# When queued work is issued around attention visits: turns and loads behind odd visits, queue rates that grow, x rows stored later

## The chip, the cores and the metric

The program runs on one core of one Trainium2 chip. The metric is the device time of one execution, in microseconds. Three runs of the kernel before took 1429.32, 1425.75 and 1430.16 us (median 1429.32). Beside them stands one profiled execution.

## What is computed

Attention with RMS-normalised queries and keys, over 8 batches of 12 heads, 448 rows of 64 numbers, followed by a feed-forward block with a squared ReLU on 3584 rows of 768 numbers:

```python
def rmsnorm(x, g):
    rms = np.sqrt(np.mean(x * x, axis=-1, keepdims=True) + 1e-06)
    return x / rms * g
q_n, k_n = (rmsnorm(q, g_q), rmsnorm(k, g_k))
scores = (1.0 / np.sqrt(q.shape[-1])) * np.matmul(q_n, k_n.transpose(0, 1, 3, 2))
scores = scores - np.max(scores, axis=-1, keepdims=True)
attn = np.exp(scores)
attn = attn / (np.sum(attn, axis=-1, keepdims=True) + 1e-09)
attn_out = np.matmul(attn, v)
x = attn_out.transpose(0, 2, 1, 3).reshape(3584, 768)
h = np.maximum(x @ w_in, 0.0)          # w_in: 768 x 2048
out = h * h @ w_out                    # w_out: 2048 x 768
```

## The kernel before

**Two streams in one program.** Attention is done for 48 pairs of heads (two heads fill the 128 partitions), six pairs for each batch. The feed-forward part (FFN) is done in four units `u`, each for two batches, that is twelve pairs: unit 0 runs while pairs 13 to 24 are attended, unit 1 with pairs 25 to 36, unit 2 with 37 to 47, and unit 3 runs alone at the end. `ffn(u)` (L925) is a generator. It issues a product, and yields its cost. `run(until)` (L1498) draws from it until the costs reach `until`, and `place(u, x)` (L1484) says how far the FFN shall be when a visit to a pair is issued. TensorE's order is thus written by hand: some FFN products, a visit, some FFN products. All engines execute in the order of issue, each its own, and so does SP, which issues all DMAs of the steady part.

**A unit.** A unit has four blocks. From unit 1 on a block begins with deep products (`deep_products`, L989, matmuls on L1018), seven products of four steps at cost 9 or 6 each, and goes on with second products (`second_products`, L1142, matmuls on L1134 and L1196), steps of cost 10 or 20. The weight pieces for the deep products (in_sb, out of in_deep in DRAM) come through `load_piece` (L873, DMA on L885) into a ring of a little over four products, about four products ahead. The weights of the second products (out_sb) come through `load_out` (L892, DMA on L895), 1.5 MB each.

**Visits.** Pairs up to 24 are visited twice each. From pair 25 on a pair is `whole` (L275): one visit, `visit_whole(i)` (L1676), which issues the scores of pair i (L433, and L444 for even i), their exponentials on ACT (`weigh`, L449, on L452) and the products of pair i - 1 with its values (L548, L569). The scores go to a few banks in turn, so a score waits until the exponential that reads its bank is done. There are three visits for each block: within the deep products, behind the first steps of the second products, and near the end of the second products. In unit 1 the odd pairs 27 and 33, in unit 2 the odd pairs 39 and 45, are at the second of these places. At pairs 25 and 37 a new unit begins, and `drain()` empties the queues ahead of the visit.

**Queued work.** What a visit needs later is put into two queues of small functions, `tasks` and `pool_tasks`. After each FFN step, `run` calls `run_tasks(most, to_send)` (L1517): it takes `most` functions (2 if the step's cost is over 10, otherwise 1) from each queue. `held` stops it: from the fourth of the deep products on for `pool_tasks`, and from the start of the seventh for `tasks`, until the second products are under way (L1190, L1207), which is just ahead of the second visit of a block. In front of each visit `run_all()` (L1523) empties both queues, held or not. Among the tasks are:

- `turn_blocks(i + 1, x)` (L362) for k (x = 1) and q (x = 0): DVE transposes (L365), for q followed by a scaling on ACT (L367), which make kT and qT of the next pair. They are put into the queue half-way between two visits (L1736), and so is `load_qk(i + 4)` (L1552), four or eight DMAs.
- `prepare(i + 3)` (L1659): the squares on ACT (L179), their sums on DVE (L192, L195), then, through `pool_tasks`, the powers and the scaling on POOL (L202, L217), and for q a way through DRAM (`store_q`, `load_blocks`), since the transposes want another layout. For even visits it is put into the queue later.
- the inversion of the sums (`invert_both`, L615), `load_v`, and `additions` (L457), six POOL operations (L471) for each pair.

**Transfers.** The DMAs of q and k go into one more queue, `transfers`, while FFN steps are drawn. `follow_transfers` (L320) sends them: 2 and one more for each eight in the queue per step in the first unit, `most` later; after the first unit `run_all` sends all that are left. `ensure` sends those that an operation needs.

**x rows.** A finished pair of a later unit, xT, is stored in DRAM (x_rows) if the forms of the unit before are still in use (`settle`, L719, DMA on L725), and loaded again by `bring` (L794). The store goes into `later`, a list that counts FFN steps (`follow_loads`, L1447): here 2.

Of the kernel before, what the change touches and what calls it, by code (L numbers as in the profile page):

```python
# [5 lines left out]

# [217 lines left out]
def program(ctx, tc, rows, v, g, wide, ones, moe_w_in, moe_w_out, out, shift):  # L224

    nc = tc.nc
# [38 lines left out]
    values, turned, through = {}, {}, {}  # L265
    weights, sums, inverse, rests, xts, forms = {}, {}, {}, {}, {}, {}
    mores, away, free, here, through_with, plan = {}, {}, {}, set(), set(), deque()
    arriving, transfers, whole_forms = deque(), deque(), set()

# [185 lines left out]
    def additions(i):  # L457

        order = [NJ, 2] if i % 2 else [2, NJ]
        for m in [1] + order:  # L460
            for e in range(2):
                pool_tasks.append(lambda m=m, e=e: add_up(i, e, m))
# [214 lines left out]
    def new_x():  # L677
        return ffn_p.tile([P, S], F32, name="xT", tag="xT", bufs=7 * NK + 4)
# [40 lines left out]
    def settle(b, c):  # L719

        u = b // 2
        if u - 1 not in through_with and (b % 2 * NPAIR + c) < 8:
            away[b, c] = dram.tile([P, S], F32, name="x_rows", tag="x_rows", bufs=8)
            xT = xts.pop((b, c))
            later.append([2, lambda: nc.sync.dma_start(away[b, c], xT)])  # L725
        arriving.append([4, (b, c)])

    def arrive(all_=False):

# [15 lines left out]
    def form_steps(u):  # L745

        b = 2 * u

        def first(c):
            some = forms[u, c] = {"T1": new_x()}  # L750
            less(nc.vector, some["T1"], xts[b + 1, c], xts[b, c])()
            some["11"] = xts.pop((b, c))

        def second(c):
            some = forms[u, c]
            some["T2"] = new_x()
            less(nc.vector, some["T2"], xts[b + 1, c + NK], some["T1"])()

        def third(c):
            some = forms[u, c]  # L760
            some["T4"] = new_x()
            less(nc.gpsimd, some["T4"], some["21"], some["T2"])()

        def fourth(c):
            some = forms[u, c]
            some["22"], some["T3"] = xts.pop((b + 1, c + NK)), xts.pop((b + 1, c))
            less(nc.gpsimd, some["T3"], some["22"], some["T3"])()

        def deeper(name):
            more = []  # L770

            def begin():
                more.append(new_more_of_words() if name in ("11", "T1", "21") else new_more())
                mores[u, name] = more[0]
                halves(0)

            def halves(n):
                c0, c1 = forms[u, 0][name], forms[u, 1][name]
                h = S // 2
                b11, b12, b21, b22 = c0[:, 0:h], c0[:, h:S], c1[:, 0:h], c1[:, h:S]  # L780
                t1, t2, t4 = [more[0][:, m] for m in range(3)]
                engine, dst, left, right = (
                    (nc.vector, t1, b12, b11), (nc.vector, t2, b22, t1),
                    (nc.gpsimd, t4, b21, t2), (nc.gpsimd, b12, b22, b12),
                )[n]
                less(engine, dst, left, right)()

            def end():
                halves(3)
                whole_forms.add((u, name))  # L790

            return [begin, lambda: halves(1), lambda: halves(2), end]

        def bring(*some):  # L794
            def load():
                for e, c in some:
                    if (b + e, c) in away:
                        xts[b + e, c] = new_x()
                        nc.sync.dma_start(xts[b + e, c], away.pop((b + e, c)))

            return load

        def lower():
            for c in range(NK):
                forms[u, c]["21"] = xts.pop((b, c + NK))

        def needs(c):
            return {(b + e, n) for e in range(2) for n in (c, c + NK)}

        def wait(n):  # L810
            return [(0, (), None) for _ in range(n)]

        upper = [{(b + e, c) for e in range(2)} for c in range(NK)]
        steps = [(2, upper[0], bring((0, 0), (1, 0))), (5, upper[1], bring((0, 1), (1, 1)))]
        steps += wait(4) + [(6, (), lambda: first(0)), (8, (), bring((0, 2), (0, 3)))] + wait(2)
        steps += [(9, (), lambda: first(1)), (11, (), bring((0, 4), (0, 5)))]
        steps += [(0, (), s) for s in deeper("11")]
        steps += [(12, upper[2], lambda: first(2)), (0, (), lower)]
        for c in range(NK):
            steps += [  # L820
                (13 + 2 * c, needs(c), lambda c=c: second(c)),
                (14 + 2 * c, needs(c), lambda c=c: third(c)), (0, (), lambda c=c: fourth(c)),
            ]
            for name in (["T1", "21"], ["T2", "22"], [None, "T3", "T4"])[c]:
                steps += [(0, (), s) for s in deeper(name)] if name else [MARK]
        return steps
# [671 lines left out]
    def run(until):  # L1498
        nonlocal spent, slowly
        slowly = True  # L1500
        while spent < until:
            cost = next(stream)
            spent += cost
            if deep_to_make:
                deep_to_make.popleft()()
            make_sum()
            follow_loads()
            end_join()
            while first and late and late[0] <= spent:
                late.popleft()  # L1510
                convert()
            arrive()
            follow_plan(2 if first else 1)
            most = 2 if cost > COST_OUT else 1
            run_tasks(most, 2 + len(transfers) // 8 if first else most)

    def run_tasks(most, to_send=0):  # L1517
        for name, some in (("others", tasks), ("pool", pool_tasks)):
            for _ in range(0 if name in held else min(len(some), most)):
                some.popleft()()  # L1520
        follow_transfers(to_send)

# [151 lines left out]
            tasks.append(lambda: load_blocks(i, 1))  # L1674

    def visit_whole(i):  # L1676
        run_all()
        if shift:
            attend_all(i - 1)
            if i <= last:  # L1680
                weigh_slots(i, 1)
        else:
            if i % 2 == 0:
                both_denominators(i - 2)
            for n in range(NJ):
                attend(i - 1, (n,))
                forget(i - 1, (n,))
                if i <= last:
                    score(i, n)
                    weigh(i, n)  # L1690
            if i % 2:
                attend(i - 1, (NJ,))
                forget(i - 1, (NJ,))
            join_halves(i - 1)
            if i % 2 == 0:
                tasks.append(lambda: invert_both(i - 2))
                if i <= last:
                    score(i, NJ)
                    weigh(i, NJ)
            if i <= last:  # L1700
                additions(i)
        if shift or i % 2:
            prepare(i + 3)
        else:
            tasks.append(lambda: tasks.append(lambda: prepare(i + 3)))
        if i <= last:
            tasks.appendleft(lambda: load_v(i))
# [7 lines left out]
    with tc.manual_schedule(engines=ENGINES):  # L1715
# [8 lines left out]
        for i in range(len(pairs) + 1):  # L1724
            for n in range(1 if whole(i) else VISITS):
                at = i * VISITS + n - VISITS - unit
                if at < 0:
                    visit_alone(i, n)
                    continue
                u, x = divmod(at, unit)  # L1730
                if x == 0:
                    u, x = u - 1, unit
                run(place(u, x - (1 if whole(i - 1) else 0.5)))
                if i < last:
                    for some in (1, 0) if whole(i) else (1 - n,):
                        turn_among(i + 1, some)  # L1736
                    if n or whole(i):
                        tasks.append(lambda i=i: load_qk(i + 4))
                    if n and first and x > 1 and not shift:
                        denominators(i - 1)  # L1740
                run(place(u, x))
                if x == unit:
                    drain()
                    stream, spent, first = ffn(u + 1), 0, u < 0
                    if shift:
                        run(COST if first else LATER)
                    elif first:
                        run(COST_IN + 1)
                slowly = x < unit
                if whole(i):  # L1750
                    visit_whole(i)
                else:
                    visit_among(i, n)
# [35 lines left out]
```

## Time and profile before

| | us |
|---|---|
| runs: median (lowest to highest) | 1429.32 (1425.75 to 1430.16) |
| profiled execution, its own time | 1431.84 |
| its span, first to last instruction | 1430.0 |
| TensorE matmuls in 0 to 100 us (attention alone) | 89.5 |
| TensorE matmuls in 100 to 510 us (unit 0) | 394.5 |
| TensorE matmuls in 510 to 849 us (unit 1) | 332.4 |
| TensorE matmuls in 849 to 1177 us (unit 2) | 318.1 |
| TensorE matmuls in 1177 to 1430 us (unit 3, no attention) | 246.8 |

The granted clock of TensorE was 0.989 over the span. A line such as `PE bank L433 <- ACT wT L452: 9.7, 5, 2.2` reads: TensorE, writing a bank at line 433, waited for ACT's instruction of line 452 that wrote wT; 9.7 us in total, 5 times, the longest 2.2 us. A line of a timeline has the start, the length, the engine, the line, the operation, the tile written and the tiles read, the number of instructions merged, and in brackets the idle time ahead of it and what ended that. In a table of stretches each row has the stretch, its length, the busy time of TensorE's matmuls, of its weight loads, of DVE, ACT and POOL, each with its number of instructions, then the granted clock, the share of the DMA engines that was busy, and GB/s. The chain that ended last gives 82% of the span to TensorE.

### The profile page before, as it was taken

How to read it: one execution, taken by the hardware profiler on the slowest of the kernel's cores; microseconds unless marked ns; L12 is line 12 of the kernel's file. 1: busy time of each engine (PE TensorE's matmuls, PEld its weight loads, DVE VectorE, ACT ScalarE, POOL GpSimd, SP SyncE). 2: the span in 40 equal slices, each digit the busy share in tenths (PEclk: the TensorE clock that was granted, in tenths of full speed). 3: DMA queues.
4: the chain of work that ended last, by engine and by line, in shares of the span. 5: the costliest groups of instructions: out<-in, count | busy, mean ns of one | idle time of the engine just before them, and what ended most of it. 6: DMA issues, size and time to landing. Idle time of an engine off the chain costs nothing.

```text
span 1430.0 us, 19473 instructions
## 1 busy us (share of the span) xinstructions
PE 1381.3 (97%) x6336; PEld 851.7 (60%) x6336; DVE 836.7 (59%) x1675; ACT 587.0 (41%) x1126; POOL 781.6 (55%) x778
## 2 busy tenths in 40 slices
PE   7998999999999998999999998999999999999998
PEld 3333444444444466585856766577675858778694
DVE  4997566987888754355445764345544565254444
ACT  6765466646656243442343423344243303221220
POOL 5666755655564966466574877546663654030311
PEclk9999999999999999999999999999999999999999
DMA  5555746867849874382646657364541716234132
GB/s 145 151 148 153 197 101 167 246 177 197 257 120 274 261 212 130 74 270 67 199 131 202 166 141 246 70 203 127 179 138 33 268 63 243 101 113 172 45 144 80
DMA packets 378931, 229.15 MB, mean 160 GB/s; under 512 B 271940, under 2 KB 347588, under 8 KB 374724
## 3 DMA queue, kind: packets, MB, share of 16 engines
q1 hardware_dynamic: 378528, 227.75, 54.7%
q8 instruction: 52, 0.85, 0.2%
q14 instruction: 59, 0.48, 0.1%
q10 hardware_dynamic: 292, 0.07, 0.0%
HBM read 172.49 MB, written 55.25 MB: 159 GB/s over the span
## 4 chain that ended last, share of the span: by engine, by line
PE 82%; DVE 5%; POOL 3%; DMA 3%; ACT 2%; issue 2%; SPq 2%; DVEq 0%; POOLq 0%; ACTq 0%
PE bank L1196 30%; PE bank L1018 24%; PE bank L1134 5%; PE bank L964 5%; PE bank L444 4%; PE bank L433 4%; PE bank L548 4%; PE bank L534 4%; PE bank L583 1%; POOL sum L471 1%; PE bank L609 1%; ACT wT L452 1%; DVE out_sb L1326 1%; PE bank L600 1%; PE bank L569 1%
## 5 line engine op out<-in xcount | busy, mean ns | idle before, releaser
L1018 PE MATMUL bank<-xT,in_sb 128*128 128x224 f32 x1344 | 290.4, 355 | 8.5 <-DMA in_sb<-in_deep 8.5
L1253 DVE TENSOR_TENSOR acc<-acc,bank 128x384 f32<-128x384 f32 x324 | 173.7, 550 | 179.2 <-PE bank L1196 156.6
L1196 PE MATMUL bank<-out_sb,hid 128*128 128x384 f32 x768 | 271.7, 491 | 3.7 <-DVE acc L1253 3.0
L1018 PEld LDWEIGHTS bank<-xT,in_sb 128*128 128x128 f32 x1344 | 253.9, 191 | 20.3 <-POOL sums L1120 6.3
L202 POOL TENSOR_TENSOR rr<-ms,minus_half 128x8 f32<-128x8 f32 (+1 forms) x96 | 147.3, 1535 | 121.8 <-DVE ms L195 104.2
L1196 PEld LDWEIGHTS bank<-out_sb,hid 128*128 128x128 f32 x768 | 145.7, 191 | 109.1 <-issue 7.2
L1196 PE MATMUL bank<-out_sb,sums 128*128 128x384 f32 x576 | 206.5, 490 | 2.0 <-DVE acc L1253 1.9
L452 ACT ACTIVATE wT<-bank,rr 128x448 f32<-128x448 f32 x288 | 164.1, 631 | 103.7 <-PE bank L444 56.1
L1003 DVE TENSOR_TENSOR hid<-hid,bank 128x224 f32<-128x224 f32 x312 | 111.4, 383 | 108.1 <-PE bank L1018 104.5
L1196 PEld LDWEIGHTS bank<-out_sb,sums 128*128 128x128 f32 x576 | 107.5, 190 | 87.2 <-issue 5.0
L964 PE MATMUL bank<-xT,in_sb 128*128 128x448 f32 x336 | 131.9, 546 | 0.1
L1071 POOL TENSOR_TENSOR hid<-hid 128x448 f32<-128x448 f32 x24 | 27.4, 1140 | 167.7 <-DVE hid L1003 154.7
L471 POOL TENSOR_TENSOR sum<-sum,wT 128x448 f32<-128x448 f32 (+1 forms) x96 | 111.8, 1185 | 8.7 <-ACT wT L452 8.1
L444 PE MATMUL bank<-qT,kT 64*128 64x448 f32 (+1 forms) x492 | 104.3, 582 | 5.2 <-ACT part L452 3.2
L964 PEld LDWEIGHTS bank<-xT,in_sb 128*128 128x128 f32 x336 | 62.1, 190 | 69.0 <-issue 59.8
L471 POOL TENSOR_TENSOR sum<-wT 128x448 f32<-128x448 f32 x48 | 57.1, 1200 | 71.7 <-ACT wT L452 70.8
L1075 ACT ACTIVATE hid<-hid 128x448 f32<-128x448 f32 x96 | 54.9, 572 | 98.2 <-DVE hid L1003 57.1
L433 PE MATMUL bank<-qT,kT 64*64 64x448 f32 x552 | 85.7, 559 | 9.7 <-ACT wT L452 9.7
L1134 PE MATMUL bank<-out_sb,hid 128*128 128x384 f32 x256 | 87.6, 488 | 0.0
L367 ACT ACTIVATE qT<-qT,g 128x448 f32<-128x448 f32 x34 | 22.7, 667 | 147.7 <-DVE qT L365 147.7
L548 PE MATMUL bank<-wT,vt 64*64 64x448 f32 x576 | 79.5, 557 | 0.0
L444 PEld LDWEIGHTS bank<-qT,kT 64*128 64x128 f32 (+1 forms) x492 | 35.6, 169 | 66.1 <-issue 39.8
(135 smaller groups left out, 2031.2 us busy)
## 6 DMA issues: line engine op xcount, KB each, us to landing
out_sb<-out_forms SPq DMA_DIRECT2D x24, 1536.0 KB, 9.8
in_sb<-in_deep SPq DMA_DIRECT2D x64, 384.0 KB, 4.2
in_sb<-in_deep SPq DMA_DIRECT2D x80, 256.0 KB, 3.8
words<-in_moe_w_in_dram SPq DMA_DIRECT2D x32, 384.0 KB, 3.7
words<-in_moe_w_out_dram SPq DMA_DIRECT2D x32, 384.0 KB, 3.5
out_forms<-out_sb SPq DMA_DIRECT2D x8, 1536.0 KB, 6.7
qk<-in_q_dram SPq DMA_DIRECT2D x96, 96.0 KB, 2.7
qk<-in_k_dram SPq DMA_DIRECT2D x96, 96.0 KB, 2.6
```

The source lines that it names most:

```text
L202: self.nc.gpsimd.tensor_tensor(out=self.rr[i][:, x, 0 : self.count(i)], in0=ms, in1=self.minus_half.to_broadcast(list(ms.shape)), op=ALU.pow,)
L433: nc.tensor.matmul(sc[ds(half * D, D)], lhsT=turned[i, 1][ds(e * D, D), ds(m * P + half * D, D)], rhs=turned[i, 0][ds(e * D, D), :], start ...
L444: nc.tensor.matmul(sc[some], lhsT=turned[p, 1][r, keys], rhs=turned[p, 0][r, :], start=True, stop=True,)
L452: nc.scalar.activation(new_weights((i, m), e), sc, AF.Exp, scale=rows.rr[i][:, 1, 2 * m + e : 2 * m + e + 1],)
L471: nc.gpsimd.tensor_tensor(out=sums[i, e][some], in0=left[some], in1=weights[key_of(i, m), e][some], op=ALU.add)
L548: nc.tensor.matmul(bank[ds(e * D, D), :], lhsT=values[i][keys, n, e, :], rhs=weights[(i, n), e][keys], start=n == 0, stop=n == NJ - 1 and ...
L964: nc.tensor.matmul(ps, lhsT=w_sb[:, IN.index(left), c, :], rhs=forms[u, c][right], start=first and c == 0, stop=c == NK - 1, skip_group_ch ...
L1003: nc.vector.tensor_tensor(out=quarter(name, n), in0=quarter(base, n), in1=ps, op=ALU.add)
L1018: nc.tensor.matmul(ps, lhsT=left, rhs=right, start=start, stop=stop, skip_group_check=True)
L1134: nc.tensor.matmul(ps, lhsT=hid[a].rearrange("p t e s -> p t (e s)")[:, t, ds(NT * P, P)], rhs=w_sb[t][:, 2 * a + half, :], start=(a, t) = ...
L1196: nc.tensor.matmul(ps, lhsT=lefts[left][:, t, ts(tt, P)], rhs=w_sb[t][:, OUT.index(right), :], start=first and t == 0, stop=t == 1, skip_g ...
L1253: nc.vector.tensor_tensor(out=acc, in0=acc, in1=ps, op=ALU.add)
```

## The change

Four things are edited. Functions for the turns and the load of a coming pair become `partial` objects that carry the pair's number; `visit_whole` takes those of its own pair out of `tasks` ahead of `run_all()` if the pair is odd, and puts them back at the head of the queue when the visit is issued. `run_tasks` takes one more function for each five in a queue. Transfers go at the first unit's rate in all units. The store of an x row waits for four steps in place of two, or goes ahead of its load if that comes first.

```diff
-    arriving, transfers, whole_forms = deque(), deque(), set()
+    arriving, transfers, whole_forms, unsaved = deque(), deque(), set(), {}
...
             away[b, c] = dram.tile([P, S], F32, name="x_rows", tag="x_rows", bufs=8)
-            xT = xts.pop((b, c))
-            later.append([2, lambda: nc.sync.dma_start(away[b, c], xT)])
+            unsaved[b, c] = xts.pop((b, c))
+            later.append([4, lambda: save(b, c)])
         arriving.append([4, (b, c)])
+
+    def save(b, c):
+        if (b, c) in unsaved:
+            nc.sync.dma_start(away[b, c], unsaved.pop((b, c)))
...
                     if (b + e, c) in away:
+                        save(b + e, c)
                         xts[b + e, c] = new_x()
                         nc.sync.dma_start(xts[b + e, c], away.pop((b + e, c)))
...
             most = 2 if cost > COST_OUT else 1
-            run_tasks(most, 2 + len(transfers) // 8 if first else most)
+            run_tasks(most, 2 + len(transfers) // 8)
 
     def run_tasks(most, to_send=0):
         for name, some in (("others", tasks), ("pool", pool_tasks)):
-            for _ in range(0 if name in held else min(len(some), most)):
+            for _ in range(0 if name in held else min(len(some), most + len(some) // 5)):
                 some.popleft()()
         follow_transfers(to_send)
...
     def visit_whole(i):
+        late = [some for some in tasks if i % 2 and getattr(some, "args", None) == (i,)]
+        for some in late:
+            tasks.remove(some)
         run_all()
...
             if i <= last:
                 additions(i)
+        tasks.extendleft(reversed(late))
         if shift or i % 2:
             prepare(i + 3)
...
                 if i < last:
-                    for some in (1, 0) if whole(i) else (1 - n,):
-                        turn_among(i + 1, some)
-                    if n or whole(i):
-                        tasks.append(lambda i=i: load_qk(i + 4))
+                    if whole(i) and not shift:
+                        tasks.append(partial(lambda i: turn_blocks(i + 1, 1), i))
+                        tasks.append(partial(lambda i: turn_blocks(i + 1, 0), i))
+                        tasks.append(partial(lambda i: load_qk(i + 4), i))
+                    else:
+                        for some in (1, 0) if whole(i) else (1 - n,):
+                            turn_among(i + 1, some)
+                        if n or whole(i):
+                            tasks.append(lambda i=i: load_qk(i + 4))
```

`shift` is a second form of the program for large gains g; the profiled execution ran the form without it.

More of the change, by code (lines that the diff above doesn't have):

```diff
@@ L3 @@
 from copy import copy
+from functools import partial
 from itertools import cycle
```

## The prediction

> **What bounds the kernel now.** I read the page's busy row first, then TensorE's waits, then the stretches of single visits, and last the order of ACT and DVE inside the worst visit.
>
> ```profile
> PE 1381.3 (97%) x6336; PEld 851.7 (60%) x6336; DVE 836.7 (59%) x1675; ACT 587.0 (41%) x1126; POOL 781.6 (55%) x778
> ```
>
> TensorE is the bound, and 1430.0 - 1381.3 = 48.7 us is all that waiting can give back, plus whatever TensorE loses by running slowly after a wait. Its waits over the whole span:
>
> ```profile
> PE bank L433 <- ACT wT L452: 9.7, 5, 2.2
> PE bank L1018 <- DMA in_sb<-in_deep: 8.5, 2, 6.0
> PE bank L1196 <- DVE acc L1253: 5.0, 5, 1.5
> ```
>
> The first row is the scores of whole visits waiting for the exponentials that free their banks: five waits. The second is two waits for weight pieces, 2.4 us at 549 and 6.0 us at 883. The third lies before 510 us, in the first FFN unit. Next, stretches of single visits (length, busy us of TensorE, weight loads, DVE, ACT and POOL with counts, granted clock, DMA share, GB/s):
>
> ```profile
> 504.92:514.91 9.99, 8.08 (x57) 2.64 (x56) 3.96 (x8) 4.14 (x7) 9.83 (x11) 0.83 0.47 96
> 567.11:577.36 10.25, 8.08 (x57) 2.81 (x56) 2.62 (x6) 5.33 (x10) 6.78 (x6) 0.83 0.38 82
> 617.94:623.58 5.64, 5.64 (x58) 2.80 (x56) 2.04 (x6) 3.42 (x7) 3.78 (x4) 1.00 1.11 364
> 732.71:740.79 8.08, 6.38 (x57) 2.35 (x56) 3.08 (x7) 4.42 (x8) 5.28 (x5) 1.00 0.47 100
> 904.98:915.23 10.25, 8.08 (x57) 2.84 (x56) 2.62 (x6) 5.33 (x10) 6.81 (x6) 0.83 0.40 85
> 1070.62:1078.70 8.08, 6.38 (x57) 2.35 (x56) 3.08 (x7) 4.39 (x8) 5.28 (x5) 1.00 0.30 60
> ```
>
> These are odd visits, with the same 56 matmuls each: pairs 25, 27, 29, 33, 39 and 45. Pair 29 is clean at 5.64 us; 27 and 39 take 10.25, 33 and 45 take 8.08, and 25 takes 9.99. 31, 35, 41, 43 and 47 are also clean (5.61 to 5.70), 37 takes 6.18, and every even visit takes 6.5 to 6.6 without a wait. The slow four are exactly the odd ones placed behind the first products of a second stage, where the `held` flag has kept tasks back. Inside pair 27's visit, ACT:
>
> ```profile
> 567.83 0.53 ACT L179 ACTIVATE squares<-qk 128x384 f32<-128x384 f32 x1
> 568.97 0.52 ACT L179 ACTIVATE squares<-qk 128x384 f32<-128x384 f32 x1 [0.62 <-DVE ms L192]
> 571.50 0.67 ACT L367 ACTIVATE qT<-qT,g 128x448 f32<-128x448 f32 x1 [2.00 <-DVE qT L365]
> 572.07 1.14 ACT L452 ACTIVATE wT<-bank,rr 128x448 f32<-128x448 f32 x2
> ```
>
> and TensorE:
>
> ```profile
> 569.65 0.92 PE L433 MATMUL bank<-qT,kT 64*64 64x448 f32 x4
> 572.74 0.83 PE L433 MATMUL bank<-qT,kT 64*64 64x448 f32 x2 [2.17 <-ACT wT L452]
> ```
>
> The first scores are in their banks by about 569, but the exponentials stand behind the scaling of qT (L367), which waits 2.00 us for DVE's transposes (L365), which wait for the squares' sums (L192). TensorE runs out of banks for 2.17 us, and what follows runs at a granted clock of 0.83 in that stretch. Pair 33's gap is 1.70 us and its clock stays at 1.00.
>
> **Change part by part.** The profiled execution took 1431.84 us, with a span of 1430.0, so 1.8 us lie around it; the three timed runs have a median of 1429.32, 2.5 us lower. I work out a difference and apply it to both.
>
> *Turns and loads behind odd visits.* At pairs 27, 33, 39 and 45 two transposes (0.65 and 0.60), one scaling (0.67) and the load of pair i+4 (four DMAs, about 0.5 us of SP each) are issued behind the visit. At 25 and 37 the queue is drained ahead of the visit, and at the other odd visits the turns have already gone, so nothing moves there. With L367 gone, pair 27's first exponential can start at 569.50, when the second square ends, not 572.07: 2.13 us behind the visit's first matmul (567.34 to 569.46), as against 1.77 in clean pair 29 (618.18 to 619.95). The gap should go, and the slow clock with it. For 33 and 45 the only square ends at 734.63, 1.7 us into the visit, which is clean. Gain: 2 x (10.25 - 5.64) + 2 x (8.08 - 5.64) = 9.2 + 4.9 = **14.1 us**. If squares stay ahead and cost 0.4 us each at 27 and 39, it is 13.3.
>
> A rule that speaks against counting all of this: the Trainium skill, "TensorE: Matmul & The Clock Gate", Part 1, puts the drop to half rate behind an idle window of about 3.4 us. By that, gaps of 1.7 to 2.2 us would not slow anything and only the gaps would come back, 7.7 us; the row shows a clock of 0.83 with a gap of 2.17, so I go by the row.
>
> The moved work falls into the second stage behind the visit. DVE idles 0.73 us before an addition there (L1253), so two transposes of 0.64 overrun by between 0 and 0.55 us; four visits lose 0 to 2.2, and I take 1.1. The next reader of qT is a visit some 18 us later. What would stand behind the late scaling on ACT is only copies; if the cover on DVE were absent, 4 x 1.28 = 5.1 us would be lost.
>
> *Growing rates for queued tasks.* Of work nothing is added. Between visit 26 and the hold there are ten steps. At one task each, those were the load of v, the inversion and its five followers, the deferred preparation, the preparation and its buffer: both squares were left for the front of visit 27. With one more task for each five in the queue, the inversion's followers leave in pairs, the preparation's nine tasks start at step eight, and both squares leave in the last three steps, in the deep products, where ACT is free. This makes the first part's 14.1 safer. The same should take turns out of the front of visit 25: the excess there is 9.99 - 5.64 = 4.35, bounds 0 and 4.35; I take 2.2, since its q rows arrive only about 504 and the turn can't come much before.
>
> Against it: tasks reach DVE and POOL closer together. DVE then stands in front of TensorE's evictions. The nearest row is DVE's wait for POOL before L632, 5.5 us in 4 waits, the longest 1.4, none of which costs TensorE anything today. POOL's chain (copies, the product L628) moves forward by about as much (one addition, 1.13 us, goes ahead of it), so the wait should stay. Bounds: a gain of 3.2 in the first unit's visits (5.26, 4.40 and 4.07 at 366, 307 and 429, where a clean one takes 3.52) to a loss of 0.64, one transpose, in each of 23 whole visits, 14.7. I take a loss of 2.5, nearer to the first, because only a queue of five or more moves faster, which is two to four steps a visit.
>
> *Growing rates for transfers.* After the first unit, two transfers and more go per step, in place of one or two. The row that matters is SP's own order before the wait at 549:
>
> ```profile
> 527.15 5.27 SPq L324 DMA_DIRECT2D qk<-in_k_dram  x4
> 532.92 3.64 SPq L324 DMA_DIRECT2D qk<-in_q_dram  x4
> 536.61 3.30 SPq L324 DMA_DIRECT2D qk<-in_k_dram  x4
> 540.01 1.72 SPq L324 DMA_DIRECT2D q_rows<-qk  x3
> 543.18 1.90 SPq L324 DMA_DIRECT2D qk<-q_rows  x4
> 545.12 1.02 SPq L375 DMA_DIRECT2D vt<-in_v_dram  x2
> 546.18 1.34 SPq L382 DMA_DIRECT2D lasts<-in_v_dram  x2
> 547.62 2.44 SPq L885 DMA_DIRECT2D in_sb<-in_deep  x5
> ```
>
> Visit 26 flushes 19 transfers ahead of the weight pieces, which reach SP at 547.62 and are waited for until 551.7. Issued earlier, the 19 still precede those pieces, so SP's total ahead of them is the same; only SP's idle time (3.7 us on L1018 between 525 and 549) could be filled, and in it the DMA engines are nearly full (0.86 from 515 to 530). Value: 0. Bounds: both waits vanish, with their slow clock (six L1018 and four L1196 behind the gap take 4.36 us where warm ones take 6 x 0.19 + 4 x 0.32 = 2.4, by 13.00 us for 68 and 20.64 us for 64 in the chain, so 2 us each): -(2.4 + 2.0) - (6.0 + 2.0) = -12.4; or the six blocks that have none get one like 549's: +6 x 4.4 = +26.
>
> *x rows stored later.* 24 stores, SP 0.38 us each. Ten of them held SP for 24 us waiting for L688 and L628; two more steps (0.6 us each) shorten that. No TensorE wait hangs on these ten, and at 550.14 and 887.6 the stores come behind the awaited pieces: 0, bounds -1 and +1 (a later store keeps its buffer and what is behind it in that list two steps longer).
>
> Sum: -14.1 + 1.1 - 2.2 + 2.5 = **-12.7**. 1429.3 - 12.7 = **1416.6 us**; a profiled execution about 1419.
>
> **Rivals.** *Only the gaps come back* (the clock of 0.83 has another cause): 2 x (2.17 + 1.70) = 7.7 and nothing net elsewhere, 1421.6. For: pair 25's gap of 1.91 already has the slow clock while 33's 1.70 hasn't, so the gap is no clean switch. Against: no whole visit without a gap is slow.
>
> *Given back on DVE and POOL*: the loss reaches its bound, -14.1 - 2.2 + 1.1 + 14.7, 1428.8. For: POOL is 55% busy with 1.1 us operations in one line. Against: TensorE waits for neither after 510 us.
>
> *The other side: q and k transfers ahead of weight pieces.* Place: SP, deep products of the eight blocks from 515 to 1110 us. A transfer issued a step sooner stands longer on what it depends on (SP waits 81.1 us for squares already, 48.9 for q rows, in sequence with the pieces). Price 4.4 us a block, as at 549; from four such blocks on it decides, and with six the time is 1416.6 + 26 = 1443. Against: pieces are asked for four products ahead, some 16 us, and in six of eight blocks this slack holds.
>
> *That it does nothing*: the moved tasks might all have left before odd visits. The transposes at 570.29 and 735.43 lie inside two of them, so for four visits this is excluded.
>
> **How the numbers follow.** Forecast 0.60, its own range 1406 (all of visit 25's excess, no loss to the queues and the wait at 549 gone: 1429.3 - 14.1 - 4.35 - 4.4) to 1422 (nothing at 25, twice the loss and more to the queues); only gaps 0.14; given back 0.12; transfers 0.14. Times within 0.3% (4.3 us, about what a measurement of this kernel can tell from no change) are 1425 to 1433.6. Faster: 0.60 + 0.14 and a little of the third, 0.75; same 0.11; slower 0.14. The range goes down to 1404, where both piece waits vanish too, and up to 1432, which leaves out the transfer rival.
>
> **What would show it.** Visits 27, 33, 39 and 45 at 5.6 to 6.1 us with no TensorE wait on L452 and a clock of 1.00; L365 and L367 behind those visits' exponentials; visit 25 nearer 8. Wrong: a second row of waits at L1018 on in_sb, or at L1196 or L1018 on DVE or POOL after 515 us.

## The result, and the profile after

The changed kernel takes 1426.18 us (median of 22 runs, 1421.62 to 1431.52), the one before 1429.92 us in the same comparison (22 runs, 1425.75 to 1434.27). The ratio is 0.9978, with a 95% interval of 0.9967 to 0.9988: 3 to 4 us faster, where 12.7 had been forecast. The profiled execution took 1425.5 us, with a span of 1423.4; it stands 6.3 us below the profiled execution of before, 2.6 more than the medians differ. Single runs spread over 8.5 us before and 9.9 us after the change.

The line numbers of the changed kernel are one higher up to the edit of `settle` and six higher from `bring` to `run_tasks`: L452 is now L453, L179 L180, L688 L689, L1003 L1009, L1018 L1024, L1196 L1202, L1253 L1259. TensorE's busy row from the page:

```profile
PE 1377.7 (97%) x6336; PEld 850.8 (60%) x6336; DVE 841.4 (59%) x1675; ACT 587.6 (41%) x1126; POOL 784.3 (55%) x778
```

TensorE's waits over the span, those of the start left out:

```profile
PE bank L1202 <- DVE acc L1259: 7.3, 6, 2.2
PE bank L445 <- ACT qT L368: 3.8, 2, 2.5
...
PE bank L1024 <- DMA in_sb<-in_deep: 2.8, 2, 1.7
PE bank L1024 <- DVE hid L1009: 2.7, 4, 0.8
PE bank L1024 <- ACT part L1013: 2.3, 4, 0.6
...
PE bank L1024 <- DVE hid L1019: 1.4, 3, 0.5
...
PE bank L434 <- ACT wT L453: 0.8, 1, 0.8
```

The row that led before, scores waiting for exponentials (9.7 us), is down to 0.8, and the waits for weight pieces are down from 8.5 to 2.8. In their place stand rows that were small or absent: the second products of unit 0 waiting for DVE's additions (5.0 before), scores waiting for qT (0.8 before), and deep products waiting for DVE and ACT to empty their banks, three rows with 6.4 us together that had none.

The stretches of the visits to pairs 25, 27, 33, 39 and 45, and last of the whole of unit 0, in the same columns as in the prediction. The second fence is unit 0 in the kernel before:

```profile
515.76:522.95 7.19, 6.38 (x57) 2.27 (x56) 3.80 (x6) 3.82 (x7) 7.11 (x8) 1.00 0.38 90
573.52:579.16 5.64, 5.64 (x57) 2.97 (x56) 0.00 (x0) 3.40 (x7) 1.81 (x3) 1.00 0.44 87
736.81:742.42 5.61, 5.61 (x57) 2.90 (x56) 1.19 (x3) 2.91 (x6) 2.82 (x4) 1.00 0.40 80
903.20:908.82 5.62, 5.62 (x57) 2.95 (x56) 0.00 (x0) 3.40 (x7) 2.25 (x3) 1.00 0.52 109
1066.56:1072.17 5.61, 5.61 (x57) 2.90 (x56) 1.19 (x3) 2.92 (x6) 2.84 (x4) 1.00 0.41 85
105.61:515.76 410.15, 391.94 (x1338) 176.18 (x1334) 301.96 (x532) 211.68 (x407) 248.93 (x208) 0.98 0.69 189
```

```profile
104.56:504.92 400.36, 386.47 (x1338) 174.66 (x1334) 302.50 (x529) 212.11 (x407) 247.65 (x207) 0.99 0.71 193
```

All four odd visits are clean, at a clock of 1.00, and the visit to pair 25 went from 9.99 to 7.19. But unit 0, between the same two matmuls, took 400.36 us before and takes 410.15 now. By the two rows, 4.3 us of these 9.8 are longer waits of TensorE, and 5.5 are longer busy time of the same matmuls (386.47 to 391.94 us) at a lower granted clock: in the changed kernel it is 0.50 from 375.94 to 379.35 us and from 481.76 to 488.58 us, behind waits of 2.45 and 1.76 us that take 0.78 and 0.69 us in the kernel before.

**A ledger by the same matmuls.** All kernels here issue the same 6336 matmuls at the same places of the hand-written order, so time can be compared between the same two matmuls of two profiled executions. "Pieces" are the two stretches in which TensorE waited for weight pieces (from the end of visit 26 or 38 to the same matmul behind the wait), "rest" is what is left of units 1 and 2 when the pieces and the six visits to 25, 37, 27, 33, 39 and 45 are taken out.

| us between the same matmuls | before | changed | difference |
|---|---|---|---|
| attention alone, up to 105 us | 101.70 | 102.76 | +1.1 |
| unit 0 | 400.36 | 410.15 | +9.8 |
| visits 25 and 37 | 16.16 | 12.83 | -3.3 |
| visits 27, 33, 39 and 45 | 36.66 | 22.46 | -14.2 |
| pieces | 47.22 | 39.31 | -7.9 |
| rest of units 1 and 2 | 551.44 | 559.49 | +8.1 |
| unit 3 | 266.67 | 266.67 | 0.0 |

The expected gain is there, to a tenth of a microsecond, and 18 us are given back in two rows. The first row is no effect: it lies between 101.4 and 102.8 us in the traces of all kernels of this document. The table holds one execution of each kernel and adds up to -6.4 us, where the medians differ by -3.7.

### The profile page after: what moved, and what is told of

It is laid out like the page before. It is cut to its first block, busy times and chain, and to the rows that moved or that the text cites. A ratio compares the mean times of both kernels' runs of the same rounds, so it can differ in the third digit from the quotient of the medians.

```text
span 1423.4 us, 19419 instructions
## 1 busy us (share of the span) xinstructions
PE 1377.7 (97%) x6336; PEld 850.8 (60%) x6336; DVE 841.4 (59%) x1675; ACT 587.6 (41%) x1126; POOL 784.3 (55%) x778
## 4 chain that ended last, share of the span: by engine, by line
PE 63%; POOL 3%; DVE 2%; DMA 2%; issue 2%; SPq 1%; ACT 1%; DVEq 0%; POOLq 0%; ACTq 0%
PE bank L1202 25%; PE bank L1024 20%; PE bank L1140 5%; PE bank L549 4%; PE bank L434 4%; PE bank L445 2%; PE bank L970 1%; POOL sum L472 1%; PE bank L535 1%; DMA in_sb<-in_deep 1%; PE bank L610 1%; PE bank L570 1%; DMA out_sb<-out_forms 0%; DVE acc L1259 0%; SPq L325 0%
## 5 line engine op out<-in xcount | busy, mean ns | idle before, releaser
L1024 PE MATMUL bank<-xT,in_sb 128*128 128x224 f32 x1344 | 289.5, 354 | 5.1 <-DMA in_sb<-in_deep 2.8
L1202 PE MATMUL bank<-out_sb,hid 128*128 128x384 f32 x768 | 271.0, 489 | 7.5 <-DVE acc L1259 5.8
L1259 DVE TENSOR_TENSOR acc<-acc,bank 128x384 f32<-128x384 f32 x324 | 173.0, 548 | 157.4 <-PE bank L1202 137.7
L1024 PEld LDWEIGHTS bank<-xT,in_sb 128*128 128x128 f32 x1344 | 252.4, 190 | 17.6 <-ACT wT L453 5.6
L453 ACT ACTIVATE wT<-bank,rr 128x448 f32<-128x448 f32 x288 | 164.1, 631 | 137.3 <-PE bank L434 74.3
L1202 PEld LDWEIGHTS bank<-out_sb,hid 128*128 128x128 f32 x768 | 144.5, 190 | 113.1 <-DVE acc L1259 9.8
L1202 PE MATMUL bank<-out_sb,sums 128*128 128x384 f32 x576 | 206.1, 490 | 1.7 <-DVE acc L1259 1.5
L1009 DVE TENSOR_TENSOR hid<-hid,bank 128x224 f32<-128x224 f32 x312 | 111.4, 384 | 87.8 <-PE bank L1024 83.5
L1202 PEld LDWEIGHTS bank<-out_sb,sums 128*128 128x128 f32 x576 | 107.7, 190 | 86.3 <-issue 4.2
L193 DVE TENSOR_REDUCE ms<-squares 128x8 f32<-128x512 f32 (+1 forms) x68 | 41.8, 615 | 64.5 <-ACT squares L180 64.5
L445 PEld LDWEIGHTS bank<-qT,kT 64*128 64x128 f32 (+1 forms) x492 | 36.7, 170 | 71.1 <-issue 40.4
L1024 PE MATMUL bank<-more,in_sb 128*128 128x224 f32 x288 | 75.2, 355 | 3.2 <-DVE hid L1009 1.8
L434 PE MATMUL bank<-qT,kT 64*64 64x448 f32 x552 | 76.1, 541 | 0.8 <-ACT wT L453 0.8
```

The costliest lines, as they stand in the source:

```text
L434: nc.tensor.matmul(sc[ds(half * D, D)], lhsT=turned[i, 1][ds(e * D, D), ds(m * P + half * D, D)], rhs=turned[i, 0][ds(e * D, D), :], start ...
L445: nc.tensor.matmul(sc[some], lhsT=turned[p, 1][r, keys], rhs=turned[p, 0][r, :], start=True, stop=True,)
L453: nc.scalar.activation(new_weights((i, m), e), sc, AF.Exp, scale=rows.rr[i][:, 1, 2 * m + e : 2 * m + e + 1],)
L1009: nc.vector.tensor_tensor(out=quarter(name, n), in0=quarter(base, n), in1=ps, op=ALU.add)
L1024: nc.tensor.matmul(ps, lhsT=left, rhs=right, start=start, stop=stop, skip_group_check=True)
L1202: nc.tensor.matmul(ps, lhsT=lefts[left][:, t, ts(tt, P)], rhs=w_sb[t][:, OUT.index(right), :], start=first and t == 0, stop=t == 1, skip_g ...
```

## Experiments

The theory with which I began, G, says that the growing task rates bring both losses. Its first rival, X, is that unit 0 lost through the later x rows or by chance. Each ratio below is to the kernel before on the same chip.

**Without growth.** The changed kernel, with

```diff
-            for _ in range(0 if name in held else min(len(some), most + len(some) // 5)):
+            for _ in range(0 if name in held else min(len(some), most)):
```

> The changed kernel with the growth of the task rates taken out (turns behind odd visits, transfer rate and x rows stay). Theory G (growth packs DVE and POOL and costs about 10 us in unit 0 and 8 us of short waits in the deep products): unit 0 as before within 1 us, visits 27, 33, 39 and 45 still near 5.7 to 6.1 us, no L1018 waits on DVE or ACT, time about 1410, ratio to before 0.985 to 0.990. Rival X (unit 0 lost through the later x rows or is another execution's chance): unit 0 stays 8 to 10 us longer, time about 1424, ratio 0.996.

Measured: 1415.19 us against 1428.5, ratio 0.9912 (0.9892 to 0.9932). Unit 0 took 402.39 us and the rest of units 1 and 2 551.66. Three of the four edits are kept, the later x rows among them, and most of the loss in unit 0 and all of it in the rest of units 1 and 2 is gone: X falls.

**Turns and loads behind odd visits, alone.** The kernel before with the edits of `visit_whole` and of the loop that fills the queue, nothing else.

> The kernel before with nothing but the turns and loads behind odd visits. The first step of the prediction says -13.3 to -14.1, ratio 0.990 to 0.991, with the two waits for weight pieces (2.4 and 6.0 us) still there and both squares ahead of visits 27 and 39. Rival (only with the squares gone as well, by the growing rates, do the visits get clean): visits 27 and 39 keep a gap of about 1 us and the slow clock, together -8, ratio 0.994.

Measured: 1414.49 us, ratio 0.9912 (0.9889 to 0.9934). The rest of units 1 and 2 is 551.44, as before to the hundredth, so the moved work costs nothing where it lands. Visits 33 and 45 take 5.61 us, 27 and 39 take 5.88: together 13.7 less than before. ACT in the visit to pair 27:

```profile
567.00 0.53 ACT L180 ACTIVATE squares<-qk 128x384 f32<-128x384 f32 x1
568.15 0.52 ACT L180 ACTIVATE squares<-qk 128x384 f32<-128x384 f32 x1 [0.62 <-DVE ms L193]
568.58 2.37 ACT L453 ACTIVATE wT<-bank,rr 128x448 f32<-128x448 f32 x4
```

Both squares are still ahead, but with the scaling of qT out of the way the first exponential starts as the second square ends, and four follow each other without a gap. The rival, that the squares have to go as well, falls: they cost 0.24 us a visit (5.88 against 5.64).

**Growth alone.** The kernel before with the growing task rates.

> The kernel before with nothing but the growing task rates. Theory G: unit 0 about 10 us longer with L1196 waiting on L1253 and L444 on L367, new short L1018 waits in units 1 and 2 (8 us), odd visits shorter by part of their excess (squares gone, turns still ahead: 2 to 6 us in all): 1438 to 1446, ratio 1.006 to 1.011. Rival X: unit 0 unchanged, time 1425 to 1430, ratio 0.997 to 1.000.

Measured: 1435.43 us, ratio 1.0049 (1.0034 to 1.0065): slower, a little less than the expected 1.006. The profiled execution is the fastest of the twelve, 1427.76 us, so its parts add up to less than the kernel before, and only the rows that agree between kernels can be read from it: unit 0 408.90 us, the rest 559.46, near those of the changed kernel. The four odd visits lose 11.5 us here too, not the 2 to 6 that were expected: at 27 and 39 the squares have left, and though the turns are still ahead, DVE has made both transposes before the visit's first matmul (at 571.42 and 571.99, with the matmul at 572.54) and the visits are clean (5.6 us); 33 and 45 take 7.0. So the two edits reach for the same time, and the growth added little to what the turns had brought.

**Growth after unit 0 only.** The changed kernel, with

```diff
-            for _ in range(0 if name in held else min(len(some), most + len(some) // 5)):
+            for _ in range(0 if name in held else min(len(some), most + (0 if first else len(some) // 5))):
```

> The changed kernel with growing task rates after unit 0 only. Theory G: unit 0 as before, units 1 and 2 as in the changed kernel, so 1426.2 - 10 = 1416, ratio 0.990. Rival X: unit 0 still long, 1425, ratio 0.997.

Measured: 1414.12 us, ratio 0.9904 (0.9884 to 0.9924); unit 0 400.61 us, the rest 559.56. The two losses are separate, each where the growth acts.

**Which queue.** The growth for one of the two queues at a time:

```diff
+            for _ in range(0 if name in held else min(len(some), most + (len(some) // 5 if name == "others" else 0))):
...
+            for _ in range(0 if name in held else min(len(some), most + (len(some) // 5 if name == "pool" else 0))):
```

> The changed kernel with the growth on the general queue alone, the POOL queue at its old rate. Theory G-split: the general queue brings the short L1018 waits of units 1 and 2 (squares and their sums, and what else goes to ACT and DVE, in the deep products; 8 us, all of it here) and the L444 waits on L367 in unit 0 (about 3.5 us); POOL's queue brings the L1196 waits. So unit 0 at 404 us, units 1 and 2 outside the marked visits at 559.5 us, time 1420, ratio 0.994. Rival P (all loss is POOL's, whose operations in a row slow DVE): unit 0 as before, units 1 and 2 at 551.5, time 1408 to 1412.

> The changed kernel with the growth on the POOL queue alone. Theory G-split: unit 0 longer by 5 to 6 us in L1196 waits on L1253 and L1426, units 1 and 2 outside the marked visits as before (551.5 us), pair 27 and 39 at 5.9 us: time 1420, ratio 0.994. Rival P: unit 0 longer by 9 to 10, units 1 and 2 by 8: as the changed kernel, 1426.

Measured: growth of the general queue 1426.6 us, 0.9988 (0.9975 to 1.0); of POOL's queue 1414.68, 0.9904 (0.9886 to 0.9921). Unit 0 409.19 and 400.55 us, the rest 562.43 and 551.54. Both theories of these runs miss: I had divided the loss of unit 0 between the queues, the rival gave POOL all of it. POOL's growing queue costs nothing, the general queue everything. Without POOL's growth beside it the general queue's rest is even 2.9 us above the changed kernel's, which stays unexplained.

**Transfers alone.** The kernel before with `2 + len(transfers) // 8` in all units.

> The kernel before with the transfers at the first unit's rate in all units, nothing else. The prediction had 0 for it, bounds -12.4 and +26. With turns behind odd visits alone the two waits for weight pieces already shrank by 5.9 us in the profiled execution, so the transfer rate may have no share in it: theory N, 1427 to 1430, both waits within 1.5 us of those before. Theory T: it takes the burst of 19 off and both waits shrink, -4 to -9, 1421 to 1425.

Measured: 1427.41 us, ratio 0.999 (0.9977 to 1.0003): no difference that can be told; pieces 45.7 us where before had 47.2, in the slowest of its twelve executions (1432.78 us). Theory T, in which this edit shrinks the waits for pieces, finds nothing here to rest on.

**What the general queue does to whom.** The waits of ACT in units 1 and 2 of the changed kernel, two rows of the list:

```profile
ACT squares L180 <- POOL xT L689: 47.1, 8, 11.8
...
ACT squares L180 <- DVE ms L193: 14.2, 14, 2.4
```

The first row is not in the list of before. The squares of a coming pair are written into a buffer that is shared with the inverses of the pair being finished (`tag="squares"`, L1665 and L641 of before), and L689 is the product that reads the inverses. At the old rates the two are far enough apart that no such wait shows. At growing rates the squares are issued too soon behind that product, and ACT, which executes in order, stands still. Pair 27's first square left in the deep products, as the prediction said, and waited there 3.31 us for L689 (it starts at 554.27). What such a wait does in the changed kernel around 616 us, ACT, DVE and TensorE in turn:

```profile
615.25 0.52 ACT L180 ACTIVATE squares<-qk 128x384 f32<-128x384 f32 x1 [2.00 <-POOL xT L689]
615.68 0.33 ACT L1013 COPY hid<-bank 128x224 f32<-128x224 f32 x1
```

```profile
615.80 0.55 DVE L193 TENSOR_REDUCE ms<-squares 128x6 f32<-128x384 f32 x1 [2.82 <-ACT squares L180]
616.39 0.17 DVE L196 TENSOR_SCALAR ms<-ms 128x6 f32<-128x6 f32 x1
616.47 0.61 DVE L1019 TENSOR_TENSOR hid<-hid,bank 128x448 f32<-128x448 f32 x1
```

```profile
617.14 0.65 PE L1024 MATMUL bank<-more,in_sb 128*128 128x224 f32 x2 [0.48 <-DVE hid L1019]
618.39 0.65 PE L1024 MATMUL bank<-more,in_sb 128*128 128x224 f32 x2 [0.61 <-DVE hid L1009]
```

ACT waits 2.00 us for L689, with the copy that empties a bank (L1013) behind it. DVE's sum waits 2.82 us for the square, with two evictions (L1019, L1009) behind it. TensorE then waits for those banks. This is theory B; its rival D is that the work is simply too dense.

To tell them apart, the inverses got a buffer of their own; one x buffer fewer made the room, and a control has the missing x buffer alone:

```diff
-        inverse[i] = io.tile([P, S], F32, name="inverse", tag="squares", bufs=1)
+        inverse[i] = io.tile([P, S], F32, name="inverse", tag="inverse", bufs=1)
...
-        return ffn_p.tile([P, S], F32, name="xT", tag="xT", bufs=7 * NK + 4)
+        return ffn_p.tile([P, S], F32, name="xT", tag="xT", bufs=7 * NK + 3)
```

> The changed kernel with the inverses in a buffer of their own, so that the squares of the pair after next don't share one with them (one x buffer fewer makes the room). Theory B: the loss in units 1 and 2 comes from squares that are issued so soon behind the product that reads the inverse (L689) that ACT and, through the sums, DVE stand still with TensorE's evictions behind them. Then units 1 and 2 outside the marked visits fall from 559.5 to 552 or 553 us, time 1419. Rival D: it is the density of work on DVE and ACT itself; then they stay at 558 to 560, time 1426.

> The control for the run with own buffers: the changed kernel with one x buffer fewer and nothing else. Both theories: as the changed kernel, 1426, units 1 and 2 outside the marked visits 559 to 560 us; if it is longer, that much of the other run is the missing buffer's.

Measured: own buffer 1418.89 us, ratio 0.9917 (0.9895 to 0.9938); control 1424.3, 0.9961 (0.9945 to 0.9977). The rest of units 1 and 2 is 553.94 us with the own buffer and 559.60 in the control; unit 0 is 409.95 and 412.03, long in both. ACT's wait for L689 is gone from the list, and of TensorE's waits on DVE and ACT one of 0.8 us is left there. The two medians differ by 5.4 us. Theory B stands for units 1 and 2: 5.7 of the 8.1 us are the shared buffer's. It does not account for unit 0, nor for the 2.5 us that stay.

**Squares and sums at the old rate.** The changed kernel, with the squares, their padding and their sums marked as `slow`. A marked function ends the additional ones of a step, so what stands behind it in the queue waits too. The loop:

```diff
+            more = most + len(some) // 5
+            for n in range(0 if name in held else min(len(some), more)):
+                if n >= most and hasattr(some[0], "slow"):
+                    break
+                some.popleft()()
```

> The changed kernel, in which squares, their padding and their sums never leave the queue as the additional functions of a step. If these alone bring the loss (theory B, and for unit 0 the order of sums ahead of the feed-forward part's own additions on DVE): units 1 and 2 outside the marked visits 551.5 to 553 us and unit 0 400 to 403, time 1409 to 1412. If the loss in unit 0 has another source in the general queue (turns, inversions, the way of q through DRAM): unit 0 stays at 408 to 410, time 1418.

Measured: 1409.46 us, ratio 0.9857 (0.9836 to 0.9878), the fastest of all. Unit 0 402.67 us, so 7.5 of its 9.8 are gone; the rest of units 1 and 2 is 554.98, above the expected 551.5 to 553. Of the 3.5 us that are left there, 2.2 lie in the visits to 29, 35 and 41, which take 6.36 us here and 5.6 in the kernel before. ACT's row for L689 is still 39.1 us in units 1 and 2 (10 waits), while TensorE's waits on DVE and ACT behind visit 25 are down from 6.4 to 1.1 us. This speaks for a cost that arises only where sums and evictions are issued right behind ACT's wait.

For unit 0, DVE's longest row of waits between its first and last matmul, in the kernel before, the changed one and this one:

```profile
DVE ms L192 <- ACT squares L179: 19.4, 11, 3.4
```

```profile
DVE ms L193 <- ACT squares L180: 44.2, 18, 5.8
```

```profile
DVE ms L193 <- ACT squares L180: 20.9, 12, 3.4
```

In unit 0 `prepare` puts no padding between a square and its sum. At the old rate the step between them was the padding; with two functions a step they are issued together, and DVE waits for the square, 25 us more in all, with additions and weight forms behind it. DVE is busy there for 302.5 of 400.4 us, so it has little room to catch up. The row goes with the loss in every trace: in the five kernels whose general queue grows in unit 0 it is 40 to 46 us and unit 0 takes 409 to 412, in the eight others 19 to 21 us and 400 to 403. That it is this wait, and not another result of the same order, is likely but not shown: no run changes the padding of unit 0 alone.

**Growth only where a unit begins.** The changed kernel, with growing rates in the steps ahead of the visits to 25 and 37 alone:

```diff
+            for _ in range(0 if name in held else min(len(some), most + (len(some) // 5 if hurry else 0))):
...
+                if x == unit:
+                    hurry.add(1)
                 run(place(u, x - (1 if whole(i - 1) else 0.5)))
...
                 run(place(u, x))
+                hurry.clear()
```

> The changed kernel with growing rates only in the steps ahead of the visits to pairs 25 and 37, where a unit begins. Theory: keeps the 13.7 us of the four odd visits, and gets the 2.8 and 0.5 us at 25 and 37 with none of the loss: unit 0 at 400 to 402.5 us, 1411 to 1413, ratio 0.987 to 0.989. Rival: the visit to 25 stays at 9.9, 1415.

Measured: 1412.74 us, ratio 0.9874 (0.9854 to 0.9894), as expected: visits 25 and 37 at 6.79 and 5.64 us, unit 0 400.97, the rest 552.02. The rival falls.

The ledger of all kernels, us between the same matmuls of one profiled execution each. A row of it doesn't stand for the median of its kernel, above all not for growth alone, profiled in its fastest execution, and transfers alone, profiled in its slowest:

| | unit 0 | 25, 37 | 27, 33, 39, 45 | pieces | rest |
|---|---|---|---|---|---|
| before | 400.4 | 16.2 | 36.7 | 47.2 | 551.4 |
| changed | 410.2 | 12.8 | 22.5 | 39.3 | 559.5 |
| without growth | 402.4 | 14.5 | 23.0 | 41.7 | 551.7 |
| turns and loads alone | 402.2 | 16.1 | 23.0 | 41.3 | 551.4 |
| growth alone | 408.9 | 12.8 | 25.2 | 40.2 | 559.5 |
| growth after unit 0 | 400.6 | 15.6 | 22.5 | 38.0 | 559.6 |
| growth, general queue | 409.2 | 12.8 | 22.5 | 41.5 | 562.4 |
| growth, POOL's queue | 400.6 | 16.1 | 23.0 | 46.4 | 551.5 |
| transfers alone | 401.4 | 16.2 | 36.7 | 45.7 | 552.0 |
| own buffer | 410.0 | 12.9 | 22.5 | 41.1 | 553.9 |
| one x buffer fewer | 412.0 | 12.8 | 22.5 | 38.3 | 559.6 |
| growth where a unit begins | 401.0 | 12.4 | 23.0 | 44.0 | 552.0 |
| squares at the old rate | 402.7 | 12.5 | 22.5 | 36.1 | 555.0 |

## Why the prediction was wrong

*Turns and loads behind odd visits: right.* 14.1 us were forecast, 13.3 with the squares still ahead. Alone this edit brought 13.7 in its four visits and 14.0 between the medians; in the changed kernel the four visits brought 14.2. The slow clock behind the gap went with the gap, as the prediction had read from its row: the rival in which only the gaps return (7.7 us) is excluded. The 1.1 us for the moved work were 0.0.

*Growing rates for queued tasks: the step that failed.* The term was +2.5 us, and it measured +17.9 (9.8 in unit 0, 8.1 in units 1 and 2), beyond its own bound of 14.7. Two things in it were wrong. It said rightly that both squares would leave in the deep products, but it put them there at no cost "where ACT is free". It priced time on the engines and didn't ask what a square waits for: a buffer that another pair's inverses still held. The sign for unit 0 was wrong too. The three visits that the bound of a gain of 3.2 us rested on took 5.26, 4.40 and 4.07 us before and 7.38, 5.82 and 4.07 after, and the fact that in unit 0 nothing but the step itself stands between a square and its sum was not weighed. The term has no part for the clock either, which brought 5.5 of the 9.8 us there. The prediction's own sign of being wrong, waits at the deep products on DVE after 515 us, came true (4.1 us on DVE, 2.3 on ACT). I had looked for the danger at DVE's wait for POOL before L632 and at POOL's queue; with POOL's queue alone growing, nothing is lost.

*Visit 25:* 2.2 forecast, 2.8 measured. The gap in it went from 1.91 to 0.81 us, which is 1.1 of that; the other 1.7 are the slow clock that follows the gap in the trace before. Without growth the gap is still 1.89, yet that trace has no slow clock behind it and the visit takes 8.27 us.

*Pieces:* 0 forecast, -7.9 in the changed kernel's execution. The transfers, to which I had tied this row, have nearly no part in it by themselves (45.7 of 47.2 us). Most kernels in which the odd visits got shorter, or the tasks earlier, have 36 to 44 us here; POOL's growth with the turns has 46.4, though, and each figure is from one execution. What moves these two waits stays open.

*x rows:* 0 forecast. No run has that edit alone. Turns alone and turns with transfers and x rows have the same ratio, 0.9912.

By the rivals: "given back on DVE and POOL" came near (14.7 us at its bound, 1428.8), with the wrong mechanism, one transpose for each visit, and a nearness that is luck in part: its loss is 3.2 us too small, and it counted nothing for the pieces. The transfer rival did not come about.

What stays open beside the pieces: some 2.5 us of the rest of units 1 and 2 with the own buffer, and with squares at the old rate 1.3 beyond the three visits named above. Unit 0 differs by 1.9 us between the kernel before and turns alone, which issue the same there (400.4 and 402.2): that is a stretch of slow clock from 288.79 to 295.62 us (0.50), which the trace before doesn't have. Of the 2.3 us by which unit 0 with squares at the old rate lies above the kernel before, 1.5 are likewise longer busy time of the matmuls (388.00 us); its trace has such a stretch at 477 us.

## What to carry to other kernels

When queued work is to be issued sooner, look for what each function was waiting behind, not only for whether its engine is free: a shared buffer, or a step of padding between a producer and its consumer, can be the reason for the old pace, and an engine that executes in order hands such a wait to everything behind it. Two edits of opposite sign can hide in one change, and a comparison between the same matmuls of two traces shows both at once, as far as a row repeats from one execution to another. Move work out of the front of a critical stretch first; that alone was worth more here than the whole change.

## What the runs showed of the hardware

Whether the clock slows behind a gap of some 2 us is not settled by the gap's length. Before the change, the gap of 2.17 us in pair 27's visit was followed by 3.40 us at a granted clock of 0.54, and that of 1.70 us in pair 33's by 3.00 us at 1.00:

```profile
572.70:576.10 3.40, 3.36 (x20) 1.28 (x24) 0.00 (x0) 1.83 (x4) 2.20 (x3) 0.54 0.72 175
...
737.80:740.80 3.00, 2.92 (x28) 1.17 (x28) 0.00 (x0) 2.74 (x6) 1.93 (x3) 1.00 0.80 191
```

In the changed kernel a gap of 2.45 us at 373 us was followed by 3.4 us at 0.58, but one of 2.18 us at 290 us by 3.50 us at 1.00. The gap ahead of the same matmul in the visit to pair 25 is 1.89 us in two kernels: with turns and loads alone the clock fell and the visit took 9.97 us, without growth it didn't and the visit took 8.27. The gap of 1.51 us near 287 us was followed without growth by 6.82 us at 0.50, from 289.45 us on, and by 7.70 us at 1.00 in the kernel before. What decides stays open here. The slow spells themselves have one size: in the trace before, between 505 and 915 us, they last 3.41 us, once 6.83.

The Trainium skill, "TensorE: Matmul & The Clock Gate", Part 1, gives about 3.4 us both for the idle time that slows the clock and for the busy time that frees it; the second agrees with these rows, the first is longer than the gaps of 1.89, 2.17 and 2.45 us that slowed it here.
